# Routing of a mixture of experts in four parts, one per pair of batches, and x stored times its probability

## The chip, the cores and the metric

One core of one Trainium2 chip. The metric is device microseconds of one execution.

## The reference

Sliding-window causal attention (8 batches, 8 heads, 576 tokens, 64 columns a head, window 64), then a dropless mixture of eight experts with one expert per token:

```python
x = attn_out.transpose(0, 2, 1, 3).reshape(4608, 512)
logits = x @ w_gate
expert_idx = np.argmax(logits, axis=1)
probs = softmax(logits)
gate_w = probs[np.arange(N), expert_idx]
for e in range(8):
    h = np.maximum(x_sorted[lo:hi] @ w1[e], 0.0)   # 512 -> 1024
    y_sorted[lo:hi] = h @ w2[e]                    # 1024 -> 512
out = gate_w[:, None] * y
```

All data is float32. The gate is positive, so scaling a token's x by it scales its y by it.

## The kernel before, in words

**Attention.** Four pairs of batches times four groups of two heads make 16 units; each has three steps of three blocks of 128 queries, 48 steps in all. A step is spread over the loop at line 381 as a software pipeline: q and k are turned (`turned`, L233), scored (`scored`, mask L254, products L275), reduced to a maximum on DVE (L282), exponentiated on ACT (L285), turned back (`flipped`, L294), multiplied by v (`weighted`, L309) and normalised on DVE into `xss` (L318), which has two buffers, one per pair. `x_turned` (L332) turns x for the gate; `routed` (L355) adds its logits up over the four groups, and for the last group of a pair copies them into one tile for all pairs (L368). SP's queue issues the loads of q, k and v; POOL makes shifted copies of v behind them (L216, L220). At the end of a pair `x_turned` stores x to `x_dram` from ACT's queue: two DMAs of 1 MB (L340) and two of 128 KB (L346). Up to the experts, the order on each engine isn't that of the text: a scheduler puts instructions forward as their inputs are expected, with priority to those that stand first, and draws up a fixed list per engine. A tile is given its buffer again once all uses of the tile that held it have ended.

**Routing** (lines 408 to 540), once, for all 36 blocks of 128 tokens: maximum and choice per token on DVE (L448 to L454), probability (L456 to L461), ranks by two products with a triangle and with ones (L467, L468) and a scan (L470), tiles per expert (L480 to L498), positions (L505 to L520), one-hot matrices `lo` (L524) and `hi` (L526 to L530), and 36 products of them (72 passes, L533) that put token number and gate into slots; `perm_i` (L537) is the list by which rows are gathered and scattered. The routing tiles take memory that the attention has left.

**Experts** (from line 546), in the order of the text. Per expert: loads of the next expert's weights on SP (`load_w`), sums of its weights on POOL (`sums_w1`, `sums_w2`, four instructions each, L121), and one body per 256 tokens, in branches that read counts at run time (L735, L740 for an odd half, L743, L745, L747, then a loop). A body is one level of Strassen-Winograd with seven products a layer: `hidden` (L609) with sums on DVE and ReLU on ACT; `turn` (L593) and `gather` (L571, L573) for the tiles that follow; `output` (L640), which forms `hs` and `xs` on DVE (L121) and adds products times gate (L647); then `scatter` (L579, L582) and a copy of the next gates (L707). Nineteen full bodies and two plain ones (an odd half, without Strassen) run here. The last additions of a body need its last product, and a skipped branch passes on the engines' counts, each engine in the order of its own queue.

## Time and profile before

| what | value |
|---|---|
| median of 3 runs | 876.24 us (874.38 to 878.36) |
| the profiled execution | 876.49 us |
| its span, first to last instruction | 874.8 us |
| mean granted TensorE clock | 0.959 of 2.4 GHz |
| PE busy | 780.4 us (89%) |
| DVE, ACT, POOL busy | 430.0, 237.7, 307.7 us |

PE is TensorE, PEld its weight loads, DVE VectorE, POOL GpSimd, SP SyncE; a q behind the name is the engine's sequencer or queue. A float32 matmul shows as two passes. In a timeline, [n <-X] is the idle time of that engine before a row and what ended it. A busy PE is not PE at its peak, since ends of matmuls are modelled.

### The profile page before, as it was taken

The page shows a single profiled execution, that of the slowest core. Times are in us where ns is not written, and L with a number is a line of the kernel's source. Part 1 is how long each engine was busy: PE and PEld are TensorE (multiplying, and loading weights), DVE is VectorE, ACT ScalarE, POOL GpSimd, SP SyncE. Part 2 cuts the span into 40 slices and gives each one's busy share as a digit, 9 for nine tenths or more (in the row PEclk, how much of TensorE's full clock was granted, in tenths as well). Part 3 has the DMA queues.
Part 4 walks back from the last instruction along what each step waited for, and adds up shares of the span by engine and source line. Part 5 has one row for each costly group of instructions (what it writes and reads, how often), then busy time and mean ns, then how long its engine had stood idle before and what let it go on. Part 6 is the DMA issues. An engine that isn't in the chain of part 4 may idle for free. (4 is left out here: it accounts for less than half of the span.)

```text
span 874.8 us, 17497 instructions
## 1 busy us (share of the span) xinstructions
PE 780.4 (89%) x6832; PEld 664.8 (76%) x6832; DVE 430.0 (49%) x818; ACT 237.7 (27%) x606; POOL 307.7 (35%) x312
## 2 busy tenths in 40 slices
PE   7998998998981479999998999889999899999992
PEld 5775776676750478999887999779888888888992
DVE  4664665665644543444436343545444436344341
ACT  4553554553530012222111221112122111121220
POOL 3221221245000063415626522735715626621121
PEclk9998999998995689999999999999999999999997
DMA  6668667878025011015143115115215143110110
GB/s 137 152 138 232 155 155 217 216 177 245 9 89 213 0 49 50 25 50 209 50 158 111 37 49 218 49 56 191 77 31 214 49 157 113 49 45 25 50 49 23
DMA packets 140302, 94.48 MB, mean 108 GB/s; under 512 B 118032, under 2 KB 118032, under 8 KB 140178
## 3 DMA queue, kind: packets, MB, share of 16 engines
q1 hardware_dynamic: 128274, 61.90, 25.3%
q0 software_dynamic: 7040, 21.50, 7.5%
q10 hardware_dynamic: 4864, 9.44, 3.0%
q8 instruction: 75, 1.23, 0.6%
q14 instruction: 49, 0.40, 0.2%
HBM read 73.94 MB, written 20.45 MB: 108 GB/s over the span
## 5 line engine op out<-in xcount | busy, mean ns | idle before, releaser
L609 PE MATMUL hp<-xs,s 128*128 128x128 f32 x912 | 108.4, 276 | 0.5 <-DVE part L618 0.5
L640 PE MATMUL yp<-s,hs 128*128 128x256 f32 x456 | 103.4, 381 | 4.7 <-DVE hs L121 4.7
L609 PEld LDWEIGHTS hp<-xs,s 128*128 128x128 f32 x912 | 105.3, 193 | 0.7 <-DVE part L618 0.7
L640 PEld LDWEIGHTS yp<-s,hs 128*128 128x128 f32 x456 | 85.9, 190 | 19.6 <-DVE hs L121 8.3
L582 POOL DMA_INDIRECT out_dram<-y,at_s x42 | 42.5, 1011 | 163.6 <-DVEq L745 51.4
L285 ACT ACTIVATE pr<-sc,mx 128x128 f32<-128x128 f32 x288 | 79.4, 374 | 70.6 <-DVE mx L282 52.6
L121 POOL TENSOR_TENSOR s<-w 128x1024 f32<-128x1024 f32 x32 | 78.3, 2449 | 57.2 <-DMA out_dram<-y,at_s 38.3
L609 PE MATMUL hp<-xq,w 128*128 128x128 f32 x608 | 76.6, 280 | 15.4 <-DVEq L740 7.9
L609 PEld LDWEIGHTS hp<-xq,w 128*128 128x128 f32 x608 | 73.0, 196 | 21.2 <-issue 21.0
L573 POOL DMA_INDIRECT xg<-x_dram,at_g x46 | 50.3, 1094 | 79.4 <-PE tp L593 69.1
L640 PE MATMUL yp<-w,hq 128*128 128x256 f32 x304 | 71.9, 379 | 0.0
L282 DVE TENSOR_REDUCE mx<-sc 128x3 f32<-128x384 f32 x96 | 49.1, 553 | 41.8 <-PE sc L275 40.3
L216 POOL COPY vb<-va 64x520 f32<-64x520 f32 x32 | 19.7, 616 | 126.7 <-DMA va<-in_v_dram 89.5
L647 DVE SCALAR_TENSOR_TENSOR party<-yp,gates,party 128x256 f32<-128x256 f32 x76 | 34.9, 479 | 57.4 <-PE yp L640 56.2
L640 PEld LDWEIGHTS yp<-w,hq 128*128 128x128 f32 x304 | 56.3, 190 | 6.8
L616 ACT COPY part<-hp 128x512 f32<-128x512 f32 x19 | 11.1, 585 | 160.5 <-PE hp L609 160.5
L121 DVE TENSOR_TENSOR hs<-hq 128x512 f32<-128x512 f32 x38 | 45.2, 1190 | 13.2 <-ACT hq L631 13.2
L618 DVE TENSOR_TENSOR part<-hp,part 128x512 f32<-128x512 f32 x19 | 13.1, 691 | 76.3 <-PE hp L609 76.3
L294 PEld LDWEIGHTS tr<-ident,pr 128*128 128x128 f32 x288 | 34.9, 146 | 20.0 <-ACT qT L238 8.3
L294 PE MATMUL tr<-ident,pr 128*128 128x128 f32 x288 | 49.7, 288 | 0.1
L275 PE MATMUL sc<-kT,qT 64*64 64x128 f32 x1152 | 47.2, 287 | 0.1
L275 PEld LDWEIGHTS sc<-kT,qT 64*64 64x64 f32 x1152 | 33.9, 138 | 12.6 <-issue 8.6
(141 smaller groups left out, 1350.9 us busy)
## 6 DMA issues: line engine op xcount, KB each, us to landing
w<-in_moe_w_dram SPq DMA_DIRECT2D x16, 2048.0 KB, 11.3
qs<-in_q_dram SPq DMA_DIRECT2D x64, 128.0 KB, 3.2
ks<-in_k_dram SPq DMA_DIRECT2D x64, 128.0 KB, 3.1
va<-in_v_dram SPq DMA_DIRECT2D x64, 128.0 KB, 2.8
x_dram<-xs ACTq DMA_DIRECT2D x8, 1024.0 KB, 6.1
qs<-in_q_dram SPq DMA_DIRECT2D x32, 32.0 KB, 2.6
ks<-in_k_dram SPq DMA_DIRECT2D x32, 32.0 KB, 2.2
vb<-in_v_dram SPq DMA_DIRECT2D x32, 32.0 KB, 2.7
```

Source lines behind the costliest of these rows:

```text
L121: op()
L216: nc.gpsimd.tensor_copy(out=vb[0:D, i].rearrange("p j h d -> p (j h d)"), in_=va[D:P, i].rearrange("p j h d -> p (j h d)"),)
L275: nc.tensor.matmul(out_, lhsT=qT[rows, t, a * WINDOW : (a + 1) * WINDOW], rhs=rhs, start=False, stop=True, skip_group_check=True,)
L282: nc.vector.tensor_reduce(out=mx[:], in_=scs[h][:], axis=AX.X, op=ALU.max, negate=True)
L285: nc.scalar.activation(out=pr[:, m, :], in_=scs[h][:, m, :], func=AF.Exp, bias=mx[:, m : m + 1])
L294: nc.tensor.transpose(out=tr[:, m, :], in_=prs[h][:, m, :], identity=ident[:])
L573: G.indirect_dma_start(out=xg[c][:], out_offset=None, in_=x_dram[:, :], in_offset=bass.IndirectOffsetOnAxis(ap=at_g[:, c : c + 1], axis=0),)
L582: put = G.indirect_dma_start(out=out[:, :], out_offset=bass.IndirectOffsetOnAxis(ap=at_s[:, c : c + 1], axis=0), in_=ys[c][:], in_offset=N ...
L609: nc.tensor.matmul(acc[:, f, :], lhsT=a[:, g, f * P : (f + 1) * P], rhs=b[:, g, :], start=(first and f == 0 and g == 0), stop=(g == HG - 1 ...
L618: V.tensor_tensor(out=u2[:], in0=y[:], in1=p1[:], op=ALU.add)
L640: nc.tensor.matmul(acc, lhsT=a[:, f, :], rhs=b[:, f, :], start=(first and f == 0), stop=(f == HF - 1), skip_group_check=True,)
L647: onto = lambda out, acc, c, more: V.scalar_tensor_tensor(out=out, in0=acc, scalar=gates[:, c : c + 1], in1=more, op0=ALU.mult, op1=ALU.add)
```

## The change

- Logits stay in a tile per pair. `choose` does expert choice, gate and ranks for one pair: for three pairs in parts, one part per attention step behind `routed`, then per step one block's one-hot matrices (`place`) and one block of x times its gate (`weigh`, on ACT and POOL in turn); a running `count` per expert carries the ranks on. The last pair runs in one go, `weigh` on ACT, DVE and POOL.
- x is stored behind `weigh` instead of from `x_turned`, still from ACT's queue; gates leave the slots and the experts.
- One-hot matrices are bfloat16, the token number in two parts (high and low) as two products; `hi` is formed for all blocks at the end, from the expert starts, in two halves. Routing tiles lie beside the attention's memory, constants are made at the start.
- The first expert's second-layer weights and their sums move behind the attention; `sums_w2(e)` stands ahead of expert e, `sums_w1(e + 1)` behind its first body.
- `sums_x` takes one input of each from PSUM. The last three additions of a body (`finish`) and its scatter move to the start of the next body; behind the last expert they stand once by themselves.

```diff
+    def load_w1(e):
+        nc.sync.dma_start(out=w1s[e % NW][:], in_=w1v[e])
+    def load_w2(e):
+        nc.sync.dma_start(out=w2s[e % NW][:], in_=w2v[e])
...
+    oh_all = consts.tile([P, E, NJ], BF16, name="oh_all")
+    rkhi = consts.tile([P, NJ], F32, name="rkhi")
+    lo = consts.tile([P, 2, NJ, P], BF16, name="lo")
...
+    with tc.tile_pool(name="tmp", bufs=1) as tmp:
+        iota(e_m[:], pattern=[[1, E]], base=-E, channel_multiplier=0)
+        ids = tmp.tile([P, P], F32, name="ids")
+        iota(ids[:], pattern=[[1, P]], base=0, channel_multiplier=0)
...
+    rt = ctx.enter_context(tc.tile_pool(name="rt", bufs=1))
+    of = rt.tile([P, E, NJ], F32, name="of")
...
+    hi = rt.tile([P, NJ, NS], BF16, name="hi")
+    def starts():
+        V.tensor_scalar_add(chunks_i[:], count[:], float(P - 1))
+        V.tensor_single_scalar(chunks_i[:], chunks_i[:], P.bit_length() - 1, op=ALU.arith_shift_right)
+        V.tensor_single_scalar(odds_i[:], chunks_i[:], 1, op=ALU.bitwise_and)
+        V.tensor_single_scalar(tiles_i[:], chunks_i[:], 1, op=ALU.arith_shift_right)
+        V.tensor_tensor(out=nt[:], in0=tiles_i[:], in1=odds_i[:], op=ALU.add)
+        V.tensor_tensor_scan(out=cum[:], data0=ones[:, 0:E], data1=nt[:], initial=0.0, op0=ALU.mult, op1=ALU.add)
+        V.tensor_tensor(out=start[:], in0=cum[:], in1=nt[:], op=ALU.subtract)
+        V.scalar_tensor_tensor(
+            out=both[:], in0=start[:], scalar=float(C), in1=odds_i[:], op0=ALU.mult, op1=ALU.add
+        )
...
-            if g == NG - 1 and c:
...
+                logits = small.tile([P, E, NTB], F32, name="logits")
...
+                return choose(bg, logits)
+        def choose(bg, logits):
+            js = slice(bg * NTB, (bg + 1) * NTB)
...
+            mx = new("r_mx", NTB)
+            V.tensor_reduce(out=mx[:], in_=by_tok(logits[:]), axis=AX.X, op=ALU.max)
+            top = new("r_top", E, NTB)
+            V.tensor_tensor(out=top[:], in0=logits[:], in1=_ins(mx[:], 1, E), op=ALU.is_equal)
+            V.tensor_tensor(out=top[:], in0=top[:], in1=_inner(e_m[:], NTB), op=ALU.mult)
+            idx = new("r_idx", NTB)
+            V.tensor_reduce(out=idx[:], in_=by_tok(top[:]), axis=AX.X, op=ALU.min)
+            oh = oh_all[:, :, js]
+            V.tensor_tensor(out=oh, in0=_inner(e_m[:], NTB), in1=_ins(idx[:], 1, E), op=ALU.is_equal)
+            pe = new("r_pe", E, NTB)
+            V.tensor_tensor(out=pe[:], in0=logits[:], in1=_ins(mx[:], 1, E), op=ALU.subtract)
+            nc.scalar.activation(out=pe[:], in_=pe[:], func=AF.Exp)
+            if bg < last:
+                yield
+            ranks = ps_lg.tile([P, 2, E, NTB], F32, name="lg")
+            for i, w in enumerate((before, ones)):
+                nc.tensor.matmul(
+                    ranks[:, i], lhsT=w[:], rhs=oh, start=(i == 0), stop=(i == 1), skip_group_check=True
+                )
+            if bg < last:
+                yield
+            inc = new("r_inc", E, NTB)
+            V.tensor_tensor_scan(
+                out=flat(inc[:]), data0=flat(keep[:]), data1=flat(ranks[:, 1]), initial=0.0, op0=ALU.mult, op1=ALU.add
+            )
+            rank = new("r_rank", E, NTB)
+            V.tensor_tensor(out=rank[:], in0=inc[:], in1=_inner(count[:], NTB), op=ALU.add)
+            V.tensor_tensor(out=count[:], in0=count[:], in1=inc[:, :, NTB - 1], op=ALU.add)
+            if bg == last:
+                starts()
+            V.tensor_tensor(out=rank[:], in0=rank[:], in1=ranks[:, 1], op=ALU.subtract)
+            V.tensor_tensor(out=rank[:], in0=rank[:], in1=ranks[:, 0], op=ALU.add)
+            V.tensor_tensor(out=rank[:], in0=rank[:], in1=oh, op=ALU.mult)
+            gates[bg] = gate = new("gate", NTB)
+            V.tensor_reduce(out=gate[:], in_=by_tok(pe[:]), axis=AX.X, op=ALU.add)
+            V.tensor_scalar_add(gate[:], gate[:], 1e-9)
+            V.reciprocal(out=gate[:], in_=gate[:])
+            if bg < last:
+                yield
+            pos = new("r_pos", NTB, dt=I32)
+            with nc.allow_low_precision("integers"):
+                V.tensor_reduce(out=pos[:], in_=by_tok(rank[:]), axis=AX.X, op=ALU.add)
+            half = new("r_half", NTB, dt=I32)
+            V.tensor_single_scalar(half[:], pos[:], P.bit_length() - 1, op=ALU.arith_shift_right)
+            V.tensor_copy(out=rkhi[:, js], in_=half[:])
+            V.tensor_single_scalar(half[:], pos[:], P - 1, op=ALU.bitwise_and)
+            V.tensor_copy(out=low[:, js], in_=half[:])
+        def place(j):
+            for i in range(2):
+                V.tensor_scalar(
+                    out=lo[:, i, j], in0=lane[:], scalar1=low[:, j : j + 1], scalar2=toks[i][:, j : j + 1],
+                    op0=ALU.is_equal, op1=ALU.mult,
+                )
+        def weigh(bg, m, engine):
+            y, s = xss[bg][:, m, :], gates[bg][:, m : m + 1]
+            if engine is nc.scalar:
+                nc.scalar.activation(out=y, in_=y, func=AF.Copy, scale=s)
+            else:
+                engine.tensor_scalar(out=y, in0=y, scalar1=s, scalar2=None, op0=ALU.mult)
+        def store(bg, i):
+            t0 = (bg * BG + i) * S
+            nc.scalar.dma_start(
+                out=x_dram[t0 : t0 + SM, :].rearrange("(n p) d -> p n d", p=P),
+                in_=xss[bg][:, i * NV : (i + 1) * NV, :],
+            )
+        def store_rest(bg):
+            for i in range(BG):
+                t0 = (bg * BG + i) * S + SM
+                nc.scalar.dma_start(out=x_dram[t0 : t0 + D, :], in_=xss[bg][i * D : (i + 1) * D, BG * NV, :])
+        gates = {}
+        todo = {}
+        def after(s, routing, bg):
+            for n in range(1, 4):
+                todo.setdefault(s + n, []).append(lambda: next(routing, None))
+            for m in range(NTB):
+                at = todo.setdefault(s + 4 + m, [])
+                at.append(partial(place, bg * NTB + m))
+                at.append(partial(weigh, bg, m, G if m % 2 else nc.scalar))
+                if m in (NV, 2 * NV):
+                    at.append(partial(store, bg, m // NV - 1))
+            todo.setdefault(s + 4 + NTB, []).append(partial(store_rest, bg))
...
-                load_w(0)
+                load_w1(0)
             if s == N - NST:
                 sums_w1(0)
-                sums_w2(0)
...
-                routed((s - 3) // NST)
+                u = (s - 3) // NST
+                routing = routed(u)
+                if routing is not None:
+                    bg = units[u][0]
+                    next(routing, None)
+                    if bg < last:
+                        after(s, routing, bg)
+                    else:
+                        for m in range(NTB):
+                            weigh(bg, m, (nc.scalar, V, nc.scalar, G)[m % 4])
+                            if m % NV == NV - 1:
+                                store(bg, m // NV)
+                        store_rest(bg)
+                        for m in range(NTB):
+                            place(bg * NTB + m)
+            for op in todo.pop(s, ()):
+                op()
...
+    s1s.append(s1_of(wp, 1))
+    w2s.append(w2_of(wp, 0))
+    s2s.append(s2_of(wp, 0))
+    w1s.append(w1_of(wp, 1))
+    w2s.append(w2_of(wp, 1))
+    s2s.append(s2_of(wp, 1))
+    load_w2(0)
+    load_w1(1)
+    load_w2(1)
...
+        V.tensor_tensor(out=of[:], in0=oh_all[:], in1=_inner(both[:], NJ), op=ALU.mult)
+        with nc.allow_low_precision("integers"):
+            V.tensor_reduce(out=base[:], in_=of[:].rearrange("p e j -> p j e"), axis=AX.X, op=ALU.add)
+        V.tensor_single_scalar(odd[:], base[:], 1, op=ALU.bitwise_and)
+        V.scalar_tensor_tensor(
+            out=early[:], in0=rkhi[:], scalar=float(C + 1), in1=odd[:], op0=ALU.is_lt, op1=ALU.mult
+        )
+        V.tensor_tensor(out=at[:], in0=rkhi[:], in1=base[:], op=ALU.add)
+        V.tensor_tensor(out=at_b[:], in0=at[:], in1=early[:], op=ALU.subtract)
+        slots = ps_rt.tile([P, NS], F32, name="slots")
+        for js in (slice(0, NJ // 2), slice(NJ // 2, NJ)):
+            V.tensor_tensor(
+                out=hi[:, js], in0=_inner(at_b[:, js], NS), in1=_ins(hi_id[:], 1, NJ // 2), op=ALU.is_equal
             )
+            for j in range(js.start, js.stop):
+                for i in range(2):
+                    nc.tensor.matmul(
+                        slots[:], lhsT=lo[:, i, j], rhs=hi[:, j], start=(i + j == 0), stop=(i + j == NJ)
+                    )
+        V.tensor_scalar(out=perm_i[:], in0=slots[:], scalar1=-1.0, scalar2=float(NT), op0=ALU.mult, op1=ALU.add)
+        V.tensor_copy(out=starts_i[:, 0:E], in_=start[:])
+        V.tensor_copy(out=starts_i[:, E:], in_=cum[:, E - 1 : E])
+        V.tensor_tensor(out=halves_i[:], in0=halves_i[:], in1=starts_i[:, 0:E], op=ALU.add)
...
-            form(right_sums(V, xs, xq[:, 0, 0], xq[:, 0, 1], xq[:, 1, 0], xq[:, 1, 1]))
+            b12, b22, b21 = tps[1][:, 0:HG], tps[1][:, HG:], tps[0][:, HG:]
+            for n, (a, b) in enumerate(((b12, xq[:, 0, 0]), (b22, xs[:, 0]), (b22, xq[:, 0, 1]), (xs[:, 1], b21))):
+                V.tensor_tensor(out=xs[:, n], in0=a, in1=b, op=ALU.subtract)
...
+        yx, yw2 = (yps[0][:, h] for h in (lo_, hi_))
+        yw, yy2 = (yps[1][:, h] for h in (lo_, hi_))
+        yy, yx2 = (yps[2][:, h] for h in (lo_, hi_))
+        plus = lambda out, a, b: V.tensor_tensor(out=out, in0=a, in1=b, op=ALU.add)
...
             form(left_sums(V, hs, a11, a12, a21, a22))
-            product(x, a11, b11)
-            scaled(out=y1a[:], in_=x, scale=gates[:, 0:1])
-            scaled(out=y1b[:], in_=x, scale=gates[:, 1:2])
-            product(w, a22, t[:, 3])
-            product(x, a12, b21, False)
-            scaled(out=ys[0][:, lo], in_=x, scale=gates[:, 0:1])
+            product_y(yx, a11, b11)
+            nc.scalar.copy(out=y1[:], in_=yx)
+            product_y(yw, a22, t[:, 3])
+            product_y(yx, a12, b21, start=False)
+            nc.scalar.copy(out=ys[0][:, lo_], in_=yx)
             sums_x()
-            product(y, hs[:, 1], t[:, 1])
-            product(y2, hs[:, 2], t[:, 2])
-            onto(v2[:], y, 0, y1a[:])
-            onto(v3[:], y, 1, y1b[:])
-            onto(v3[:], y2, 1, v3[:])
-            product(w2, hs[:, 0], t[:, 0])
-            onto(ys[1][:, lo], w, 2, v3[:])
-            onto(ys[1][:, hi], w2, 1, v3[:])
-            onto(v2[:], w2, 0, v2[:])
-            product(x2, hs[:, 3], b22)
-            onto(ys[0][:, hi], x2, 0, v2[:])
+            product_y(yy, hs[:, 1], t[:, 1])
+            product_y(yy2, hs[:, 2], t[:, 2])
+            plus(v1[:], yy, y1[:])
+            plus(v3[:], yy2, v1[:])
+            V.tensor_tensor(out=ys[1][:, lo_], in0=v3[:], in1=yw, op=ALU.subtract)
+            product_y(yw2, hs[:, 0], t[:, 0])
+            product_y(yx2, hs[:, 3], b22)
+        def finish():
+            plus(v2[:], yw2, v1[:])
+            plus(ys[1][:, hi_], yw2, v3[:])
+            plus(ys[0][:, hi_], yx2, v2[:])
...
+        def body(e, last, after, full):
+            finish()
+            scatter(last)
             (hidden if full else plain_hidden)(e)
             turn()
...
-            scatter(now)
-            G.tensor_copy(out=gates[:], in_=gate_t[:, nxt])
...
         for e in range(E):
             chunks, odd, at = coming
-            if e + 1 < E:
-                if e:
-                    load_w(e + 1)
-                sums_w1(e + 1)
+            if 0 < e < E - 1:
+                load_w1(e + 1)
+                load_w2(e + 1)
+            sums_w2(e)
...
             with tc.If(chunks > 1):
                 body(e, *place(at), True)
             if e + 1 < E:
-                sums_w2(e + 1)
+                sums_w1(e + 1)
                 coming = counts(e + 1)
...
+        end = G.value_load(starts_i[0:1, E : E + 1], min_val=0, max_val=NTILE)
+        finish()
+        scatter(bass.ds(end * C, C))
```

## Rows read from the trace of the kernel before

**Rows 1.** Stages: us, then busy us (instructions) of PE, PEld, DVE, ACT, POOL; PEclk, DMA, GB/s.

```profile
100.00:120.00 20.00, 20.00 (x278) 14.46 (x277) 13.96 (x35) 11.51 (x39) 4.50 (x8) 1.00 0.69 154
...
260.70:271.00 10.30, 0.00 (x0) 0.00 (x0) 0.00 (x0) 0.00 (x0) 0.00 (x0) 0.62 1.03 399
...
313.80:858.70 544.90, 522.23 (x3521) 478.79 (x3520) 250.68 (x393) 106.76 (x199) 241.06 (x202) 1.00 0.25 86
```

**Rows 2.** Timeline, end of the attention to first expert product: start, us, engine, line, instruction.

```profile
256.42 0.37 SPq L138 DMA_DIRECT2D w<-in_moe_w_dram  x1
...
260.46 0.23 DVE L368 COPY logits<-tr 128x72 f32<-128x72 f32 x1 [1.96 <-PE tr L364]
...
271.05 0.64 DVE L448 TENSOR_REDUCE r_mx<-logits 128x36 f32<-128x288 f32 x1 [10.36 <-DMA x_dram<-xs]
...
282.16 0.46 DVE L510 TENSOR_TENSOR rank<-rank,oh 128x288 f32<-128x288 f32 x1
...
283.54 0.18 DVE L517 TENSOR_SCALAR half_i<-pos_i 128x36 int32<-128x36 int32 x1
...
284.07 4.96 DVE L524 TENSOR_TENSOR lo<-half,iota 128x4608 f32<-128x4608 f32 x1
...
296.07 10.49 PE L533 MATMUL slots<-hi,lo 128*128 128x116 f32 x72 [19.10 <-DVE hi L530]
...
306.60 0.22 DVE L537 TENSOR_SCALAR perm_i<-slots 128x58 int32<-128x58 f32 x1 [10.58 <-PE slots L533]
...
313.77 3.62 PE L609 MATMUL hp<-xq,w 128*128 128x128 f32 x16
```

**Rows 3.** Waits of the whole span: us in total, times, longest us.

```profile
POOL vb L216 <- DMA va<-in_v_dram: 89.5, 20, 9.8
...
PE sc L254 <- ACT pr L285: 9.2, 7, 3.8
...
ACT pr L285 <- DMA x_dram<-xs: 11.2, 2, 5.9
```

**Rows 4.** TensorE's waits in the expert stage, 313 to 860 us.

```profile
PE hp L609 <- DVEq L740: 7.9, 6, 1.5
...
PE yp L640 <- DVE hs L121: 4.7, 8, 0.8
...
PE hp L609 <- DVEq L745: 3.4, 4, 0.9
...
PE hp L609 <- issue: 2.5, 1, 2.5
...
PE tp L593 <- DMA xg<-x_dram,at_g: 2.3, 5, 1.0
...
PE hp L609 <- DVEq L747: 1.6, 2, 0.8
```

**Rows 5.** Line 740, sequencers' instructions: duration ns min/median/max, first and last start.

```profile
L740 PEldq EVENT_SEMAPHORE  x6: 51/51/51, 342.1 to 806.8; - x6
...
L740 DVEq EVENT_SEMAPHORE  x6: 21/21/21, 343.4 to 807.4; - x6
```

**Rows 6.** Timeline of the last body.

```profile
848.23 1.15 POOL L573 DMA_INDIRECT xg<-x_dram,at_g  x1 [0.30 <-issue]
...
849.05 0.68 DVE L121 TENSOR_TENSOR hs<-hq,hs 128x512 f32<-128x512 f32 x1
```

**Rows 7.** Line 121, by form: duration ns min/median/max, first and last start.

```profile
L121 DVE TENSOR_TENSOR xs<-xq x44: 410/420/3119, 314.6 to 850.4; 128x256 f32<-128x256 f32 x44
...
L121 POOL TENSOR_TENSOR s<-w x32: 2337/2363/2804, 172.1 to 748.5; 128x1024 f32<-128x1024 f32 x32
```

**Rows 8.** The chain that ended last, in order of time.

```profile
861.37 1.00 POOL out_dram L582
```

**Rows 9.** Line 747, the innermost branch.

```profile
L747 POOLq COMPARE_BRANCH  x6: 38/44/50, 396.7 to 866.2; - x6
```

**Rows 10.** DMA issues from 240 to 300 us: KB each, median us to landing.

```profile
x_dram<-xs ACTq DMA_DIRECT2D x2, 1024.0 KB, 8.9
```

259 lines of the change are left out of this document (80 added, 179 removed).

## The prediction

> **What bounds the kernel now.** I read first the busy time by stage, then the timeline of the stage with the idlest TensorE, then TensorE's waits in the expert stage. Three stages matter. During the attention TensorE is the full engine: 20.00 of 20 us in a steady stretch, with DVE at 13.96 and ACT at 11.51 [rows 1]. During the experts it is also the bound, 522.23 of 544.9 us at a granted clock of 1.00, that is 2.4 GHz [rows 1]. Between them lies the routing, and there TensorE has almost nothing: the last logits are written at 260.46 + 0.23 = 260.7 and the first expert product starts at 313.77 [rows 2], 53.1 us. Part of that gap is a wait without any work on any engine: from 260.70 to 271.00 all five are at 0.00 while the DMA engines are full at 399 GB/s [rows 1], and the row that ends it says that the first routing instruction (L448) waited 10.36 us for the stores of x. It needs only logits; its new tile lies where x lay. The rest is one chain: DVE builds the positions of 36 blocks of tokens, the one-hot matrices (4.96 us for 4,608 elements of the first), 72 passes on TensorE from 296.07 (10.49 us), perm_i at 306.60 [rows 2].
>
> The sum is made on the profiled execution: 876.49 us, of which 874.8 are its span. The median of the three runs is 876.24, so the two agree within 0.3 us. About 0.5% (4.4 us) is what a measurement of this kernel can tell from no change.
>
> **Routing.** The change moves the choice, the ranks and the low one-hot matrices of three of four pairs into the attention, and gives all routing tiles their own memory, so the 10.36 us go. After 260.7 the new chain is, in DVE instructions (a 72-element one taken at 0.23, as the 128x72 copy at 260.46; small ones at 0.18 as at 283.54; each with 0.04 of hand-over, as between the dependent ones there):
> - expert choice, six instructions of 72 elements: 1.6, to 262.3.
> - rank sums on TensorE: before, the slots' passes took 10.49/72 = 0.146 us; two passes and the hand-overs 0.9 (between 0.3 for the passes alone and 1.4 for four passes of 288 columns), to 263.2.
> - scan, ranks and masks 1.6, the eight small `starts` 1.7, gate 0.6, position halves 1.0: to 268.1.
> - two of nine scalings of x on DVE at 0.6 each (512 elements at the 1.08 ns of the row at 284.07), and 18 one-hot blocks of 128 elements at 0.20 (between 0.18, that of 36 elements, and 0.28, on the line from there to 0.46 for 288; nearer the low end because they are bf16): 4.8, to 272.9.
> - the correction by expert starts, 0.5 + 0.7 + four of 0.2: 274.9; the first half of hi, 1,044 elements, 1.2: 276.1. The second half lies beside TensorE.
> - slots, again 72 passes, with 58 columns for 116 and bf16: between 5.2 (half) and 10.5 (as before); I take 6, nearer to half, because columns and width both shrink: 282.1.
> So perm_i starts at 282.1 in place of 306.60: **24.5 less**. The ends of these bounds put it between 277 and 289.
>
> The Trainium skill ("TensorE: Matmul & The Clock Gate", Weight-path perf modes) says that a 128-column weight load which isn't FP32 is loaded fast, about twice as fast measured; by it the 72 passes would be nearer 4 us and the sum 2 us lower. No row shows such a load in this stage.
>
> x now goes out later, because it is scaled by the gate first: ACT takes five blocks, 3 us from about 267, so the last store is issued near 271. SP meanwhile has three weight loads in place of two behind 256.42: 6.3 MB and 2.36 MB of x at 399 GB/s end at 256.4 + 21.7 = 278.1. That is before perm_i, so it is hidden; if the chain were at its short end, the two would meet. The gather, turn and first product behind perm_i stay as they are (306.60 to 313.77).
>
> **Attention.** Three times some 20 small DVE instructions and 18 blocks, about 7.6 us a pair, 23 in all; five scalings on ACT and four on POOL a pair; two tiny TensorE products. DVE has 6 us free in 20 [rows 1], and a pair lasts 62 us, so nearly all fits in gaps; TensorE has none, so what delays its inputs counts. I take 1 us a pair, **3 more**. Bounds: 23 more if all lay in the chain, 9 less if the stores, now elsewhere, no longer hold ACT's queue at the end of a pair (stores held ACT 11.2 us in two waits, and TensorE lost 9.2 us to ACT's exponentials in seven waits [rows 3]). The iotas go to the start, where POOL also builds the mask; I leave them at nothing beside the first loads, 1 us if that cover is short.
>
> **Experts.** Twelve waits of TensorE, 7.9 + 3.4 + 1.6 = 12.9 us, name DVE's queue at a skipped branch [rows 4]. At the first of them TensorE's sequencer had passed the branch's event at 342.1, DVE, behind the last addition of the body, only at 343.4 [rows 5]; that wait is one of the 1.5 us. The change moves the three last additions and the scatter into the next body: DVE's last instruction is then ys[1]'s low half, which needs nothing of the last two products (3.8 us of work), so its queue is at the branch first. I take 0.2 a join as TensorE's own remainder: **10.5 less** (bounds 0 and 12.9). What waits for the moved additions is the scatter and nothing on TensorE before the next output.
>
> Sums of weights: the second-layer sums now run ahead of an expert, the first-layer ones behind a body's gather. Before, they ran on POOL over DVE's hs sums, and TensorE lost 4.7 us in 8 waits for hs; it lost 2.3 us to gathers counted late, since POOL passed the skipped branch only behind its sums [rows 4]. Now they begin behind a body's gather, whose last part ended at 848.23 + 1.15 in the last body, when the fourth hs (849.05) was the one running [rows 6]: **3.5 and 1.8 less** (bounds 0 and all).
>
> The row that decides what a collision costs: DVE's x sums take 0.42 us, and 3.119 when POOL's sums (2.36 each) run beside them [rows 7]. The Trainium skill ("SBUF — State Buffer", SBUF: two separate sides) states the reason: the port pair of both is an exclusive lock for a DVE instruction with two SBUF inputs against a POOL one that reads SBUF. The trace agrees. By that rule the x sums, with one input in PSUM, are now free of it, and the fourth hs isn't; and the four scalings on POOL a pair are a new owner of the lock, against DVE instructions that read SBUF twice.
>
> Dropping the gates, two ACT scalings into one copy, and the column copies: nothing, since TensorE is the bound there and ACT is at 106.76 of 544.9 by the stage's row [rows 1].
>
> **End.** The chain of work that ended last has POOL's last scatter at 861.37 + 1.00 [rows 8], but its sequencer compares the last branch only at 866.2 [rows 9]; now the skipped branch lies ahead of the last scatter. **3.5 less** (0 to 3.8).
>
> Sum: -24.5 + 3 - 10.5 - 3.5 - 1.8 - 3.5 = -40.8; 876.49 - 40.8 = 835.7, say **836 us**.
>
> **Rivals.**
> *A, the joins stay.* TensorE's own fetch of a far branch target is what costs, and DVE only ends with it. For: one gap of 2.5 us has no releaser but issue [rows 4]. Against: the sequencer's event at 342.1. Then 836 + 10.5 = 846.5.
> *B, x's buffer.* Pairs share two buffers of x. The stores of a pair stand two steps behind the first write of the pair after the next in the text; if that order held, each of two pairs would wait two steps (5.2 us each, 260.7 over 50) and a landing of 8.9 [rows 10], 19 us, 38 in all: 874, no change. Against: instructions don't run in the order of the text; the first expert's weight sums, written at step 45 of 48, began at 172.1 [rows 7], far ahead of that step.
> *C, slower: ACT stands behind POOL.* A large store waits on ACT's queue for a scaling that POOL does, and POOL waits for loads of v, up to 9.8 us at a time, 89.5 in 20 waits [rows 3]. Exponentials stand behind that store, and TensorE behind them. It turns the sign when a pair loses over 41/3 = 14 us; two stores at 9.8 are 19.6 a pair, 59 in all: 895. Against: POOL's order is also drawn up by readiness.
> *D, DVE in the chain.* All 23 us of new DVE work lie in the attention's chain: 856.
>
> **Chances.** Forecast 0.72, A 0.10, B 0.06, C 0.05, D 0.07. Faster by over 0.5%: forecast, A and D, 0.89; within: B, 0.06; slower: C, 0.05. The range takes the short ends of routing and attention below (822) and A, and most of D, above (856): 822 to 856.
>
> **What would show it.** The first routing instruction right behind 260.7; perm_i near 282; first product near 292 with 3 us from the attention; no wait on DVE's queue in TensorE's list; hs waits under 2 us; x sums at 0.45 throughout; a span end within 13 us of the last product. Wrong if logits end past 275 (B, C, D), if perm_i follows them by over 29 us, or if bodies are still over 1 us apart.

## The result and the profile after

The changed kernel takes 821.83 us (median of 4 runs, 821.27 to 822.16) beside 875.82 us (4 runs, 874.38 to 878.36): a ratio of 0.938, 95% interval 0.936 to 0.940. The profiled execution took 822.16 us, 820.5 of them span. The forecast was 836, with a range from 822; the time lies 0.2 us below it. So the direction and most of the mechanisms held, and 13.5 us more came out than were summed.

The head of the profile after (busy time by engine; granted clock in 40 slices):

```profile
span 820.5 us, 17675 instructions
...
PE 765.0 (93%) x6868; PEld 659.0 (80%) x6868; DVE 407.2 (50%) x955; ACT 239.0 (29%) x610; POOL 318.1 (39%) x305
...
PEclk9999999999997699999999999999999999999997
```

The timeline of the changed kernel over the routing, the answer to [rows 2] (start, us, engine, line, instruction, idle before):

```profile
253.98 0.23 DVE L424 COPY logits<-tr 128x72 f32<-128x72 f32 x1 [1.96 <-PE tr L419]
...
254.24 0.28 DVE L440 TENSOR_REDUCE r_mx<-logits 128x9 f32<-128x72 f32 x1
...
260.84 0.31 DVE L491 TENSOR_SCALAR lo<-lane,low,tok_a 128x128 bf16<-128x128 bf16 x1
...
266.19 2.40 DVE L603 TENSOR_TENSOR hi<-at_b,hi_id 128x1044 bf16<-128x1044 bf16 x2
...
267.49 3.64 PE L608 MATMUL slots<-hi,lo 128*128 128x58 bf16 x72 [11.42 <-DVE hi L603]
...
271.80 0.15 DVE L611 TENSOR_SCALAR perm_i<-slots 128x58 int32<-128x58 f32 x1
...
279.74 2.12 PE L669 MATMUL tp<-ident,xg 128*128 128x128 f32 x8 [8.61 <-DMA xg<-x_dram,at_g]
...
281.65 2.49 PE L686 MATMUL hp<-xq,w 128*128 128x128 f32 x16
```

The first routing instruction now stands right behind the logits, where the 10.36 us wait was. Set against the marks of [rows 1, 2], in us:

| stage | before | after | difference | forecast |
|---|---|---|---|---|
| attention, to the last logits written | 260.7 | 254.2 | -6.5 | +3 |
| logits to perm_i | 45.9 | 17.6 | -28.3 | -24.5 |
| perm_i to the first expert product | 7.2 | 9.85 | +2.7 | 0 |
| experts, first to last product | 544.9 | 526.1 | -18.9 | -15.8 |
| last product to the end of the span | 16.1 | 12.8 | -3.3 | -3.5 |
| sum | | | -54.3 | -40.8 |

TensorE's waits in the expert stage of the changed kernel, the answer to [rows 4] (us in total, times, longest):

```profile
PE hp L686 <- DVE party L715: 5.9, 7, 0.9
PE hp L686 <- PEq L817: 2.7, 6, 0.5
```

The waits for hs (4.7 us) and for gathered rows (2.3) are gone, and the joins fell from 15.4 (7.9 + 3.4 + 1.6 and the 2.5 without a releaser) to 8.6. The stage by windows, as in [rows 1] (us, busy of PE, PEld, DVE, ACT, POOL, clock):

```profile
281.65:807.73 526.08, 517.52 (x3553) 483.87 (x3552) 211.09 (x383) 95.22 (x180) 239.47 (x189) 1.00 0.27 91
```

TensorE's idle time fell from 544.94 - 522.26 = 22.7 to 8.6 us; the other 4.7 us are busy time, part of it in the first body, which ran at a granted clock of 0.98 instead of 0.93.

### The profile page after: what moved, and what is told of

Same layout as the page of the kernel before. It is cut to its first block, busy times and chain, and to the rows that moved or that the text cites. A ratio compares the mean times of both kernels' runs of the same rounds, so it can differ in the third digit from the quotient of the medians.

```text
span 820.5 us, 17675 instructions
## 1 busy us (share of the span) xinstructions
PE 765.0 (93%) x6868; PEld 659.0 (80%) x6868; DVE 407.2 (50%) x955; ACT 239.0 (29%) x610; POOL 318.1 (39%) x305
## 5 line engine op out<-in xcount | busy, mean ns | idle before, releaser
L719 PE MATMUL yp<-s,hs 128*128 128x256 f32 x456 | 101.5, 379 | 0.0
L116 POOL TENSOR_TENSOR s<-w 128x1024 f32<-128x1024 f32 x32 | 75.3, 2356 | 35.6 <-DMA xg<-x_dram,at_g 25.5
L719 PE MATMUL yp<-w,hq 128*128 128x256 f32 x368 | 86.0, 379 | 0.0
L715 DVE TENSOR_TENSOR party<-yp,party 128x256 f32<-128x256 f32 x60 | 25.4, 424 | 105.3 <-PE yp L719 67.0
L719 PEld LDWEIGHTS yp<-w,hq 128*128 128x128 f32 x368 | 68.3, 190 | 8.4
L658 POOL DMA_INDIRECT out_dram<-y,at_s x44 | 44.3, 1008 | 69.7 <-DVE y L715 55.5
L357 PEld LDWEIGHTS tr<-ident,pr 128*128 128x128 f32 x288 | 33.2, 143 | 23.6 <-ACT qT L301 6.8
L372 PE MATMUL px<-va,pT 128*64 128x65 f32 x640 | 43.4, 231 | 0.0
L502 POOL TENSOR_SCALAR xs<-xs,gate 128x512 f32<-128x512 f32 x14 | 22.1, 1587 | 47.6 <-PE lg L457 37.0
```

Source lines behind the costliest of these rows:

```text
L116: op()
L357: nc.tensor.transpose(out=tr[:, m, :], in_=prs[h][:, m, :], identity=ident[:])
L372: nc.tensor.matmul(px[a * D : (a + 1) * D, h, m, :], lhsT=pTs[h][:, m, a * D : (a + 1) * D], rhs=vt[:, h, :], start=True, stop=True, skip_ ...
L502: engine.tensor_scalar(out=y, in0=y, scalar1=s, scalar2=None, op0=ALU.mult)
L658: put = G.indirect_dma_start(out=out[:, :], out_offset=bass.IndirectOffsetOnAxis(ap=at_s[:, c : c + 1], axis=0), in_=ys[c][:], in_offset=N ...
L715: plus = lambda out, a, b: V.tensor_tensor(out=out, in0=a, in1=b, op=ALU.add)
```

## The experiments

Each kernel's time is its median. The kernel before, run beside them on the same chip, had 874.3 to 877.3 us where it ran repeatedly. Where a run changes only the experts, its attention may still start 2.2 us earlier or later than that of the changed kernel; this is told under the sixth run, and the stages are compared from perm_i on.

**1. Before, with the stores of x of the first three pairs issued by POOL.**

```
-                nc.scalar.dma_start(
+                q_ = nc.scalar if bg == B // BG - 1 else nc.gpsimd
+                q_.dma_start(
```

> The kernel before, with the stores of x of the first three pairs issued from POOL's queue in place of ACT's. Theory S (a pair's stores hold ACT's queue at the end of the pair, and their move made the attention shorter): the last logits come 8 to 10 us ahead of 260.7, the whole some 866 us. Theory W (the first expert's second-layer load and sums, which left the attention, made it): logits at 260.7 within 1.5 us, the whole 875.

864.33 us (one run), 11.2 less than the kernel before beside it. ACT's two waits of [rows 3] are gone, and TensorE's 9.2 us for exponentials are 0.2. The instructions on the logits in this kernel (duration in ns min/median/max, first and last start):

```profile
L369 DVE COPY logits<-tr x4: 232/233/235, 82.6 to 244.6; 128x72 f32<-128x72 f32 x4
L449 DVE TENSOR_REDUCE r_mx<-logits x1: 643/643/643, 256.8 to 256.8; 128x36 f32<-128x288 f32 x1
```

The last logits are copied at 244.6 where they started at 260.46: 15.9 us, more than expected. r_mx still waits 12.0 us for the last stores, so part of it is given back. These stores on ACT's queue were the dearest thing in the attention.

What held ACT was not the issuing, which takes 0.36 to 0.95 us a store. The end of the third pair in the kernel before:

```profile
198.12 0.37 ACTq L340 DMA_DIRECT2D x_dram<-xs  x1
202.21 5.67 ACTq L346 DMA_DIRECT2D x_dram<-xs  x2
207.93 1.66 ACT L285 ACTIVATE pr<-sc,mx 128x128 f32<-128x128 f32 x6 [5.27 <-DMA x_dram<-xs]
```

The second of the two small stores goes out at 207.43, 0.02 us behind the landing of the large one (207.41 by the trace). In the trace the loads of SP and the stores of ACT take eight completion semaphores in turn, and a small store waits there until the transfer ahead of it on its semaphore has landed: of the six small stores of three pairs, five go out 0.02 us behind such a landing, four of them that of a load that SP issued. Stores from POOL have semaphores of their own. Around these waits TensorE, which stood for 1.7 to 3.8 us at a time, is granted half its clock (1.2 GHz), and here it is not. Three stretches of the kernel before, and one of this kernel (us, then busy us and instructions of PE, PEld, DVE, ACT, POOL, clock):

```profile
82.25:89.07 6.82, 5.14 (x36) 3.69 (x37) 1.35 (x3) 2.85 (x9) 0.00 (x0) 0.50 0.68 162
147.11:150.51 3.40, 3.34 (x21) 2.60 (x20) 0.79 (x2) 0.91 (x3) 0.00 (x0) 0.50 0.69 154
208.55:215.36 6.81, 6.20 (x49) 4.43 (x50) 1.80 (x4) 2.24 (x8) 6.62 (x5) 0.50 0.70 164
```

```profile
30.00:240.00 210.00, 209.35 (x2942) 149.35 (x2943) 138.75 (x337) 115.31 (x363) 58.16 (x76) 1.00 0.68 170
```

TensorE is busy for 14.7 us of the three. Equal products take 1.56 us at half clock and 0.89 at full (run 6), so some 6 us of it are lost, by estimate, beside the 9.0 us of waits.

**2. Before, with expert 0's second layer loaded behind the attention.**

```
-                load_w(0)
+                nc.sync.dma_start(out=ws[0][0][:], in_=w1v[:, 0:1, :, :])
-                sums_w2(0)
+    nc.sync.dma_start(out=ws[0][1][:], in_=w2v[:, 0:1, :, :])
+        sums_w2(0)
```

> The kernel before, with the first expert's second-layer weights loaded behind the attention and their sums formed behind the first gathers, as after the change. Theory W: the last logits come 4 us or more ahead of 260.7. Theory S: the same 260.7 within 1.5 us; the first routing instruction, which waits for the stores beside 6.3 MB of weights in place of 4.2, comes up to 5 us later, the whole 875 to 881.

876.71 us (one run), no change. The last logits come 3.4 us earlier (257.0) and the first product too (310.3), but the experts use it up (548.6 us for 544.9). 2.8 of the 3.4 us are there by the logits of the first pair (83.4 for 86.2), long before the first load of weights, which the kernel before issues at 163.4. So this load is not what held the attention.

**3. Changed, with the stores of the first three pairs at the pair's end again, x unscaled.** The scaling by the probability is left out for three of four pairs, so the run has less work than the change.

```
+            if bg < last and g == NG - 1 and c:
+                store(bg, c - 1)
+                if c == NST - 1:
+                    store_rest(bg)
-                at.append(partial(weigh, bg, m, G if m % 2 else nc.scalar))
-                if m in (NV, 2 * NV):
-                    at.append(partial(store, bg, m // NV - 1))
-            todo.setdefault(s + 4 + NTB, []).append(partial(store_rest, bg))
```

> The changed kernel with x of the first three pairs stored unscaled at the end of its pair, from ACT's queue as before the change, and without its scaling: the gate is left out for three of four pairs. Theory S: the last logits come 6 to 10 us later than 254.2 although the scalings are gone. Theory W: at 254.2 or up to 3 us earlier. In both the experts stay as they are, so the whole moves by the same.

825.79 us (one run). The logits end 3.9 us later, less than expected, in spite of the work left out, and the old waits are back. ACT's wait for stores of x in this kernel:

```profile
ACT pr L348 <- DMA x_dram<-xs: 10.4, 2, 6.0
```

In the changed kernel it was 1.7 us, once. It is the place of the stores that counts: at the pair's end they stand on ACT's queue ahead of the exponentials, and TensorE waits for those.

**4. Changed, with the stores of the first three pairs issued by POOL.**

```
-            nc.scalar.dma_start(
+            (nc.scalar if bg == last else G).dma_start(
```

> The changed kernel with the stores of x of the first three pairs issued by POOL instead of ACT, all else as it is. Theory S (the 6 us that the attention gained came from stores that no longer hold ACT's queue; by now one wait of 1.7 us is left): last logits 1 to 3 us earlier, the whole 819 to 821. Rival (the gain had another source): no difference, 821 to 823.

813.74 us (4 runs), 0.931 of the kernel before (0.928 to 0.933), 8 us below the changed kernel, over twice what was expected. The copies of the logits in this kernel, as under run 1:

```profile
L424 DVE COPY logits<-tr x4: 231/232/233, 81.4 to 248.2; 128x72 f32<-128x72 f32 x4
```

The last logits come 5.8 us earlier (248.2 for 253.98); 2.1 of it lies in the start (below). So even the stores behind the scaling cost ACT's queue some 3.7 us. 2.9 us more come at the end of the program, and that part stays unexplained (last section).

The four numbers for the last logits divide the attention's term, if each is counted from the first logits product of its profile, since the starts differ for another reason (run 6). These products in the kernel before, in run 1, in the changed kernel and here:

```profile
L355 PE MATMUL lg<-xT,wg x96: 485/498/511, 27.0 to 258.9; 128*32 128x384 f32 x96
L356 PE MATMUL lg<-xT,wg x96: 486/498/510, 29.1 to 243.0; 128*32 128x384 f32 x96
L410 PE MATMUL lg<-xT,wg x96: 486/498/510, 30.0 to 252.4; 128*32 128x384 f32 x96
L410 PE MATMUL lg<-xT,wg x96: 486/498/510, 27.9 to 246.6; 128*32 128x384 f32 x96
```

Without stores on ACT's queue it is 215.5 before (244.6 - 29.1) and 220.3 after: the work that the change adds to the attention costs 4.8. With them it is 233.5 and 224.0: they cost 18.0 before and 3.7 after. 4.8 - 18.0 + 3.7 = -9.5, and the start, 3.0 later in the changed kernel's profile, makes -6.5 of it.

**5. Changed, with the routing's constants behind the mask.** (The block with the iotas moves, unchanged, behind the mask's instructions.)

> The changed kernel with the constants of the routing made behind the mask in place of ahead of it. Theory M (POOL's constants delay the mask and with it every step): the first normalised block comes at 18.0 in place of 20.9 and the whole takes 819 us. Rival (the first steps are later for another reason, such as the order of the loads or DVE's copies): no change at 822.

818.39 us (one run). The last mask instruction and the first masked products, in the changed kernel and then here:

```profile
6.71 0.78 POOL L242 TENSOR_SCALAR_AFFINE_SELECT mask<-mask 64x128 bf16<-64x128 bf16 x2
...
8.32 0.84 PE L317 MATMUL sc<-mask,ident_b 128*128 128x384 bf16 x2
```

```profile
5.10 0.78 POOL L213 TENSOR_SCALAR_AFFINE_SELECT mask<-mask 64x128 bf16<-64x128 bf16 x2
...
7.22 0.85 PE L317 MATMUL sc<-mask,ident_b 128*128 128x384 bf16 x2
```

The mask is 1.6 us earlier and the products are 1.1. The last logits come 4.4 us earlier (249.6), of which some 1.8 are the difference in the start that kernels with the attention unchanged show as well (next run).

**6. Changed, with the finish and scatter behind the hidden layer's first product.**

```
-            finish()
-            scatter(last)
+            def rest():
+                finish()
+                scatter(last)
             product(x, a11, xq[:, 0, 0])
+            rest()
```

> The changed kernel with the finishing products and the scatter of the tile before put behind the first product of the new expert's hidden layer instead of ahead of it. Theory H (what is left at the expert heads, 5.9 us in 7 waits of 0.82 for DVE's party sum, is caused by DVE having the finishing sums ahead of it in its order): these waits fall to under 2 us and the whole is 816 to 819. Rival (the party sum waits for its own input, or for the skip): the waits stay at 5 to 6 us, the whole stays at 822, or rises by up to 3 us for a later scatter.

820.10 us (4 runs, 819.61 to 823.48), no difference that can be told. TensorE's waits at the joins in this kernel:

```profile
PE hp L686 <- DVE party L716: 5.8, 7, 0.8
...
PE hp L686 <- PEq L821: 2.6, 6, 0.5
```

So the 8.6 us that the joins keep (0.82 at a join ahead of a new expert, 0.42 at another) are not the finishing sums; what they are, no run shows. The profiled execution is 1.8 us shorter than that of the changed kernel and was so by the last logits already; the attention is the same text. Its first products show it. A stretch of the changed kernel, and the same of this one (us, busy and instructions of PE first, then PEld, DVE, ACT, POOL, clock):

```profile
12.00:14.00 2.00, 2.00 (x13) 1.43 (x9) 0.70 (x2) 1.75 (x8) 1.67 (x4) 1.00 0.41 71
```

```profile
12.00:14.00 2.00, 2.00 (x25) 1.40 (x21) 1.11 (x2) 2.00 (x8) 1.54 (x4) 1.00 0.43 74
```

TensorE is busy in both, but does half as many products in the changed kernel; the first logits product is at 30.0 there and at 28.2 here. The reason is TensorE's clock, although the column says 1.00 in both: the trace's records of the granted clock begin at 19.93 us in the changed kernel and at 11.85 here, and where there is no record the column shows 1.00. Equal groups of products (start, us), in the changed kernel and then here:

```profile
17.66 1.56 PE L338 MATMUL sc<-kT,qT 64*64 64x128 f32 x24
...
22.49 0.89 PE L338 MATMUL sc<-kT,qT 64*64 64x128 f32 x24
```

```profile
9.15 1.56 PE L338 MATMUL sc<-kT,qT 64*64 64x128 f32 x24
...
15.03 0.89 PE L338 MATMUL sc<-kT,qT 64*64 64x128 f32 x24
```

The 1.56 us are those of half clock: in run 8, whose record has half clock from 20.3 to 23.7 us, the group at 21.14 takes 1.56, the one at 14.79, before it, 0.89. In the four profiles of kernels with the changed attention whose records begin at 19.1 to 20.2 us, that logits product stands at 30.0 to 30.2; in the seven whose records begin at 10.3 to 12.0 us, with no half clock up to that product, at 27.7 to 28.2. What sets it is open. Differences of 2 us between kernels with one attention are therefore not read as an edit's.

**7. Changed, with expert 1's weights loaded behind the first turn, from ACT's queue.**

```
-    load_w1(1)
-    load_w2(1)
+        nc.scalar.dma_start(out=w1s[1][:], in_=w1v[1])
+        nc.scalar.dma_start(out=w2s[1][:], in_=w2v[1])
```

> The changed kernel with the loads of expert 1's two layers moved out of SP's queue ahead of the gather and onto ACT's queue behind the first token load of the experts. Theory G (the gather of the first tile lands late, 9.85 us from the slots to the first product where it was 7.17 before, because these loads and the stores of x fill the DMA engines just then): the gather lands 1.5 to 3 us earlier, the first product comes at about 279 instead of 281.65, the whole is about 820. Rival (the gather takes its own latency, or waits for the stores of x): the first product stays within 0.5 us of 281.65, the whole stays at 822 or gets worse by a wait of expert 1 for its weights.

817.30 us (4 runs), 2.8 below run 6, which shared the chip and the start. The wait for the first gathered rows is 6.3 us instead of 8.6, and perm_i to the first product is 7.2 us again, as before. That wait in this kernel:

```profile
PE tp L667 <- DMA xg<-x_dram,at_g: 6.3, 1, 6.3
```

The 2.7 us that this stage lost were the gather beside two 2 MB loads. It now starts 34.8 us earlier (271.80 for 306.60), and so meets them.

**8. Changed, with the last routing part in memory that the attention held.** (Its six tiles are allocated behind the attention.)

> The changed kernel with the tiles of the last routing part in memory that the attention's tiles held before. Theory (memory of its own is worth something at the end, since the last part need not wait for the attention's last readers): the slots come 0.5 to 4 us later, 822.5 to 826. Rival (the last part waits for the last logits anyway): 821 to 823.

827.00 us (4 runs), 5.2 more. DVE makes everything up to the low one-hot blocks and then stands; the timeline row that ends it, and the row of its sequencer (duration in ns):

```profile
268.99 0.46 DVE L590 TENSOR_TENSOR of<-oh_all,both 128x288 f32<-128x288 bf16 x1 [6.02 <-issue]
...
L590 DVEq EVENT_SEMAPHORE  x4: 50/50/8324, 260.3 to 268.9; - x4
```

In the changed kernel this instruction ran at 260.47, ahead of these blocks. The timeline names no releaser, but the sequencer stood for 8.3 us from 260.3 on semaphores that, in the trace, the last pair's stores of x use, and the packets of these stores run to 268.2. So it waits for them, as r_mx did before [rows 2]. Memory of its own is worth 5 us even for the last part alone.

**9 to 14. The three edits in the experts, undone one by one, by pairs, and all.** The edits: F, finish and scatter in the next body (undone: at the end of the own body); O, POOL's weight sums in the new order (undone: the first layer's at an expert's head, the second layer's behind its first body); X, sums of x from PSUM (undone: from SBUF). The undoing of F, of O and of X against the changed kernel (with F the scatter behind the last expert goes too, and the columns of the slots follow):

```
-            finish()
-            scatter(last)
...
                 plain_output(e)
+            finish()
+            scatter(last)
```

```
+        sums_w2(0)
...
-            sums_w2(e)
+            if e + 1 < E:
+                sums_w1(e + 1)
...
-                sums_w1(e + 1)
+                sums_w2(e + 1)
```

```
-            b12, b22, b21 = tps[1][:, 0:HG], tps[1][:, HG:], tps[0][:, HG:]
+            b12, b22, b21 = xq[:, 0, 1], xq[:, 1, 1], xq[:, 1, 0]
```

9, F undone:

> The changed kernel with the finishing products and the scatter of a tile put back at the end of its own expert's body, as before; all else of the change stays. Theory J (this move alone took the waits behind the skipped branch and shortened the tail): the experts lengthen by 6 to 11 us (the waits of TensorE's first instruction at the joins come back to some 15 us) and the tail by 3 to 4 us, the whole is 830 to 836. Rival (the joins shrank because of the other edits in the experts, the order of the weight sums or the x sums from PSUM): the whole is 822 to 826, with the waits at the joins at 8 to 9 us.

10, X undone:

> The changed kernel with the sums of x read from SBUF again instead of PSUM. Theory X (the move to PSUM took the 4.7 us in 8 waits for the sums of the hidden layer, since a DVE sum of two SBUF tiles stands still beside POOL's sums): these waits come back, the experts lengthen by 3 to 6 us, the whole is 825 to 828. Rival (the order of the weight sums alone took them, the x sums would now be hidden): the whole is 821.5 to 823.

11, O undone:

> The changed kernel with POOL's weight sums alone in the order of before; finish and scatter stay late, sums of x from PSUM. Theory O (the new order by itself took the 4.7 us of waits for the sums of the hidden layer): the whole is 825 to 828. Rival X (they went because the sums of x no longer stand still, and the order alone is worth nothing): 821 to 824. Rival C (order and late scatter hang together both ways: POOL now reaches the scatter later): over 830, with TensorE waiting for the weight sums or the gathered rows.

12, O and X undone:

> The changed kernel with POOL's weight sums in the order of before and the sums of x read from SBUF: of the edits in the experts only the late finish stays. Theory C (each of the three edits pays only with the others: 858 us with SBUF sums under the new order because a sum of x stands still for up to 3.2 us beside POOL's sums at the expert's head): under the old order the standing sums are back at the 4.7 us of before, the whole is 825 to 830. Rival (sums from SBUF cost the 36 us under either order): over 850.

13, F and O undone:

> The changed kernel with both the finishing products and scatter at the end of the own body and POOL's weight sums in the order of before (first layer's at the expert's head, second layer's behind its first body). Theory C (the new order of the weight sums needs the late scatter: with the scatter early, POOL waits for the last tile's sums before it can make the second layer's sums of the same expert, 35.7 us of TensorE in 7 waits): these waits vanish, the joins keep some 14 us and the tail its extra 3.4, the whole is 830 to 837. Rival (the early finish costs the 58 us by itself, whatever the order): the whole stays above 860.

14, all three undone:

> The changed kernel with all three edits in the experts undone (finish and scatter at the end of the own body, weight sums in the old order, sums of x from SBUF): what is left of the change is the routing and the attention. Theory A (attention and routing gave about 32 of the 54 us, the three edits in the experts together about 22): 842 to 846. Rival (as the prediction had it: routing 24.5, attention a loss of 3): 852 to 856. Rival (the sums of x pay by themselves under the old order too, 2 us or more beyond the 839 of the run with PSUM sums): 841 to 844 with waits for the hidden sums of some 5 us against some 2.

Medians of 4 to 6 runs each:

| in place | us | against none in place |
|---|---|---|
| none | 841.46 | |
| X | 839.09 | -2.4 |
| F | 856.92 | +15.5 |
| F, X | 858.90 | +17.4 |
| O, X | 880.28 | +38.8 |
| F, O | 861.83 | +20.4 |
| F, O, X (the change) | 821.83 | -19.6 |

(O alone was not run. X alone is no difference that can be told: its runs, 838.6 to 839.6, touch those with none in place, 839.3 to 843.5.) Every expectation that undoing one edit would cost its own few us fell: it costs 37 to 58, more than all three are worth together. The first two single undoings were expected at 822 to 836 and came at 880 and 862. In time, rival C of run 11 (over 830) and the rival of run 12 (over 850) held, the latter not by its reason, since with the sums of x from PSUM (run 11) it is no faster. Runs 13 and 14 came 2 us above and 0.5 us below what their first theories gave. The waits tell why. F undone (O, X in place), waits of TensorE and of POOL:

```profile
PE yp L719 <- POOL s L116: 35.7, 7, 7.5
...
PE hp L686 <- DVEq L817: 8.1, 6, 1.8
PE hp L686 <- DVEq L822: 4.3, 5, 0.9
...
PE hp L686 <- DVEq L824: 1.7, 2, 0.9
```

```profile
POOL s L116 <- DMA out_dram<-y,at_s: 36.6, 5, 9.3
```

With the scatter at a body's end, POOL cannot begin the second layer's sums of an expert before the last tile of the expert ahead is scattered, and that expert's own output needs them. The joins are back at 14.1 us too. O undone (F, X in place), waits of TensorE, POOL and DVE:

```profile
PE hp L686 <- DVE part L695: 20.0, 5, 4.7
```

```profile
POOL s L116 <- DMA w<-in_moe_w_dram: 95.3, 6, 18.8
```

```profile
DVE y L715 <- DMA out_dram<-y,at_s: 39.7, 5, 8.7
```

Now the first layer's sums stand at the head and wait up to 18.8 us for their weights, with the late scatter behind them on POOL's queue; the next finish waits for that scatter to leave y, and DVE's sums of the hidden layer stand behind the finish. X undone (F, O in place), waits of TensorE, and the sums of x, to set against [rows 7]:

```profile
PE yp L719 <- DVE party L715: 25.0, 7, 3.6
```

```profile
L676 DVE TENSOR_TENSOR xs<-xq x44: 416/420/3249, 280.1 to 837.1; 128x256 f32<-128x256 f32 x44
```

At the expert's head POOL's sums now run beside the sums of x: in the trace 23 of 88 meet one, and the longest takes 3.249 us when it reads SBUF twice, as the 3.119 of before. In the changed kernel 5 of 88 meet one, and the longest of this form is 0.425:

```profile
L676 DVE TENSOR_TENSOR xs<-tp,xq x44: 410/415/425, 282.5 to 799.5; 128x256 f32<-128x256 f32 x44
```

With none in place the time is 841.46: what is left of the change, nearly all of it routing and attention (the experts take 542.9 us there, for 544.9 before), gives 34 of the 54 us, the three edits as a group 19.6. The end shows F by itself: from the end of the last product to the end of the span it is 15.7 us in the three runs without F (826.0 to 841.7 with none in place), and 12.7 in the three with it (845.3 to 858.0 with F and O).

**15. The edits that paid, together:** mask first (run 5), expert 1's weights late (run 7), stores from POOL (run 4).

> The changed kernel with three edits that the runs speak for: constants of the routing behind the mask, expert 1's weights loaded from ACT's queue behind the first turn, and the stores of x of the first three pairs issued by POOL instead of ACT. If the gains add (some 2 to 3 us for the mask, 2 to 3 for the gather, up to 2 for ACT's queue): 812 to 816. Rival (POOL's queue, which now carries scalings and copies of v, makes the attention wait): 818 to 825.

811.54 us (4 runs, 810.29 to 813.19), 0.925 of the kernel before (0.923 to 0.928): the fastest of all, 10.3 us below the changed kernel. Most of that is the stores. The other two add 2.2 us by the medians, less than each gave alone, but the kernel before was 3.0 us slower beside this run than beside run 4 (877.28 for 874.28), so up to 5 is possible. TensorE's wait for the first gathered rows here:

```profile
PE tp L667 <- DMA xg<-x_dram,at_g: 5.6, 1, 5.6
```

## Why the prediction was right and wrong

**Routing**, forecast -24.5 and read -28.3: right in mechanism, with two terms mis-sized. The slots' 72 passes took 3.64 us where I took 6, and DVE's chain from the logits to the start of hi 12.0 where I took 14.2. The rule named there (the Trainium skill, "TensorE: Matmul & The Clock Gate", Weight-path perf modes: a 128-column weight load that isn't FP32 is loaded fast) had given, as an estimate, nearer 4, and the trace agrees in size: 0.05 us a pass for 0.146, at a granted clock of 0.50. But columns and element type changed at once, so no run shows the weight load by itself. The low blocks took 0.22 each from start to start (18 in 4.1 us), near the 0.20 taken. Small DVE instructions start closer than their durations: r_top at 254.56 and r_pe at 254.71, each 0.23 long. The wait of 10.36 us went, as said, and run 8 shows that it is the memory: a wait for the same stores comes back when only the last tiles share.

**Attention**, forecast +3 and read -6.5: **this is the step that failed.** "I take 1 us a pair, 3 more" came near the added work (4.8 by runs 1 and 4), but the sentence's other bound, "9 less if the stores, now elsewhere, no longer hold ACT's queue", was no bound on the same quantity: it was a second effect, with rows to price it at hand, 11.2 us of ACT's waits and 9.2 of TensorE's [rows 3]. Both happened. Added, the two would have given 3 - 9 = -6, and the sum 827. That this is near the -6.5 is luck: the stores gave 18.0 - 3.7 = 14.3 and not 9, because the half clock around TensorE's waits (run 1) was in no term, and a start 3.0 us later (the iotas and TensorE's clock, runs 5 and 6) took part of it back. Of the miss of 13.5 us this step is 9.5. The lower end of the range, 822, is 836 - 5 - 9; by the bounds as they are stated, 277 for 282.1 and -9 for +3, it would have been 818.6. The iotas ahead of the mask cost 1.1 us at the products, the "1 us if that cover is short".

**Perm_i to the first product**, forecast "stay as they are", read +2.7: the transfers were summed only up to perm_i's forecast time, 278.1 against 282.1. Perm_i came at 271.80, and "the two would meet" is what happened (run 7).

**Experts**, -15.8 and read -18.9, a sum that came out nearly right from terms that were not. The joins gave 6.8 and not 10.5: only the six joins behind an expert's first body (L740) fell, from 1.4 to 1.5 us each to 0.42 to 0.52, while the seven ahead of a new expert keep 0.8 to 0.9, as six of them had before, and one had 2.49. What is left is not the finishing sums (run 6). That part stays as rival A had it, though no run shows that a branch's fetch is the cause. The hs and gather waits gave all 7.0 of which 5.3 were taken, and 4.7 us came from TensorE's busy time, which no term held. What the sum did not see is that its terms are one: F alone, credited with 10.5 and the 3.5 of the end, costs 15.5; O with X, credited with 5.3, costs 38.8. The three need each other: POOL's queue carries the sums, the scatter and the gather in one order (F and O), and in the new order its sums fall beside the sums of x (X).

The reason given for the sums of x held. By the rule on the port pair (the Trainium skill, "SBUF — State Buffer", SBUF: two separate sides) a sum with one input in PSUM is free of it. The trace agrees: beside POOL's sums 0.42 at most after, and 3.249 in the run with SBUF. The fourth hs, as forecast, isn't free; it takes up to 3.276 us now, and hides.

**End**, -3.5 and read -3.3: right, and shown by the runs without F.

**Rivals.** B, C and D did not happen: no wait on x's buffer, 2.5 us of TensorE's waits on exponentials for 9.2, and 4.8 us of added chain instead of 23.

## What to carry to other kernels

Where a change both adds work to a stage and removes a wait from it, the two are two terms to be added, not the two ends of one range. When edits move work between engines that run in order, list each engine's queue as it will stand and price the edits as a group: here each pair of three edits was a loss against none, and the three a gain. Look at which engine issues a large store, and what that store waits for: behind a store on ACT's queue stood the exponentials, and TensorE with them. And price the clock with the wait: in the attention before, stretches at half clock cost some 6 us beside 9.0 of waits, by estimate.

## What was not expected of the hardware

- Issuing the twelve stores of x of three pairs from POOL instead of ACT was worth 11.2 us in the kernel before and 8.1 in the changed one, although there the large ones took 7.2 us to land instead of 5.5. (By the profiles 3.7 us of the latter lie in the attention and 2.9 at the end; 2.1 are TensorE's clock at the start and not the stores'.) The Trainium skill ("DMA: Bandwidth & Descriptors", Issuing engines are not separate DMA queues) says that spreading issues over engines saves only the sequencer's time to issue, usually small. The issues agree: 0.36 to 0.95 us each on ACT's queue before. What was dear is another thing, the wait of a store on that queue for the landing of an earlier transfer, up to 5 us with the exponentials behind it (run 1).
- A wait of TensorE costs more than itself. With X undone its waits for DVE in the experts grew by 25.0 + 2.8 us, and the stage by 40.0 (566.1 for 526.1); its busy time there grew by 12.4 for the same products. With F undone, in the stretch from 500 to 600 us:

```profile
500.00:600.00 100.00, 83.56 (x529) 75.63 (x528) 41.22 (x57) 14.35 (x27) 44.33 (x30) 0.91 0.33 117
```

  The granted clock, 1.00 in the changed kernel there (98.70 us busy), is 0.91 on average, between the levels of 2.4 and 1.2 GHz, after waits of up to 7.5 us.
- TensorE's first products ran at half rate until 12 or until 20 us, between kernels whose attention is the same text, and the first logits product came about 2 us earlier or later with it (run 6). A clock of 1.00 in a profile's column is no reading where the trace has no record yet.
- With the stores on POOL's queue the span ends 3.1 us after the last scatter's issue (807.68 + 1.00 to 811.8), in the changed kernel 8.3 us (811.19 + 1.00 to 820.5), although POOL reaches this scatter later after its data (2.84 us of issue for 0.56). Run 15 shows the same end. What fills it is one instruction of POOL's sequencer at the kernel's last line, in the changed kernel and in run 4 (duration in ns):

```profile
L855 POOLq DRAIN  x3: 46/113/9425, 810.2 to 820.2; - x3
```

```profile
L855 POOLq DRAIN  x3: 46/113/4072, 806.7 to 811.5; - x3
```

  In the changed kernel it runs to 819.6, long after the last scatter has landed (813.8). With the stores on POOL's queue in the kernel before (run 1) it is not shorter, 8.2 us for 7.4. What it waits for is open, and it was not tried by itself.
